# Decode attention over a sliding window with a gated feed-forward: units of one head or of two heads, runs of 24 KB or 48 KB per partition

## The chip, the cores and the metric

The kernel runs on one NeuronCore of a Trainium2 chip. The metric is the device time of one execution in microseconds. Five engines work side by side, each through its own list of instructions in order: TensorE (PE; its weight loads are shown as PEld), VectorE (DVE), ScalarE (ACT), GpSimd (POOL) and SyncE (SP), which here issues the transfers between the device memory (HBM) and the on-chip memory (SBUF). The transfers run on 16 DMA engines. Matrix products land in a second on-chip memory, PSUM.

## The reference

Four batches, one new position each. The 640-wide input is normalised, and two branches of it are added to the input: attention over the last W = 2,048 cached positions (32 heads of 192, every head with its own keys and values), and a SiLU-gated feed-forward of width 1,536. All data are bf16.

```python
B, Sq, D = 4, 1, 640
Hq, Hkv, Sk, Dh = 32, 32, 8192, 192
# k_cache, v_cache: (B, Hkv, Sk, Dh); wq: (D, Hq*Dh); wo: (Hq*Dh, D); w1, w3: (D, 1536); w2: (1536, D)
W = min(4096, max(256, Sk // 4))            # 2048
xn = layernorm(x)
q = (xn @ wq).reshape(B, Sq, Hq, Dh).transpose(0, 2, 1, 3)
k = k_cache[:, :, Sk - W:, :]; v = v_cache[:, :, Sk - W:, :]
p = softmax(einsum("bhqd,bhkd->bhqk", q, k) * Dh ** -0.5)
o = einsum("bhqk,bhkd->bhqd", p, v).transpose(0, 2, 1, 3).reshape(B, Sq, Hq * Dh) @ wo
h = silu(xn @ w1) * (xn @ w3)
out = x + o + h @ w2
```

Each key and each value is used once, so some 201 MB of cache pass through the core, and 22 MB of weights.

## The kernel before

The unit of work is a head of all four batches. `cache_rows` lays 2,048 positions of four batches on 128 partitions: partition q*4+b holds 64 neighbouring positions of batch b, one run of 64x192 bf16 = 24,576 bytes. `load_k` and `load_v` (L97, L102) move 3 MB each. Three key buffers and three value buffers stand ready (`KBUFS`, `VBUFS`); each wait for a free buffer is a wait of SP, ahead of everything that SP issues later.

A head is worked in four chunks of 16 positions per partition, one chunk per slot of a schedule. `mult` (L205, DVE) multiplies keys with the broadcast query into `pr`; `adder` (L215, PE) sums 192 products to 32 with six products against the identity, into one of two PSUM tiles `ps`; `reduce_tile` (L224, DVE) sums the 32. After the last chunk a chain finds the maximum of each batch: `lmax` (L231), a transpose (L236), `gmax` and `gmq` (L241, L244), a broadcast product (L250), `negm` (L252); then ACT takes the exponentials into `z` (L256), one instruction per batch and with a mask, so that each batch's row of `z` is zero on the other batches' partitions. `pv` (L275, PE) multiplies `z` with the values in 32 products of 32 columns, which go by turns to four column groups of PE; `fold` (L288, L292) adds the groups' rows and divides by the row sum of L262 and L264. Every four heads, `ge_tr` (L298) transposes the result, and `ge_proj` (L309) adds its product with 768 rows of `wo` into `acc`. The feed-forward comes last: gate and up (`ffn_mm`, L329), SiLU (L336), `ffn_transpose` (L346), `ff` (L406).

The order is written out by hand: `sched` holds, per slot (one chunk of keys, four per head) and phase, the functions to call. PE, DVE and ACT keep the order in which instructions are emitted, except that the build moves some forward between neighbours; SP issues in the order of the calls. These lines set what this text speaks of:

```python
if h >= KBUFS:
    add(s0 - (KBUFS - 1) * NC, 0, load_k, h)
add(s0 + L + NC * (1 - VBUFS), 0, load_v, h)
...
add(end - 2, 0, ffn_load, 1)
add(end - 2, 0, ffn_load, 3)
for n in range(NF):
    add(end, 0, w2_load, n)
add(end + L + 1, 7, ffn_mm, 1)
```

With `L` = 9, a head's products with the values begin nine slots after its first chunk. The query weights `wq` pass through the value buffers before the first values do. The gate weights go into key buffers behind the last heads' keys and behind the last V; `w2` follows them.

Of the kernel before, what the change touches and what calls it, by code (L numbers as in the profile page):

```python
# [18 lines left out]
def kernel(  # L19
# [16 lines left out]
    KBUFS: int = 3,  # L36
    VBUFS: int = 3,
    PBUFS: int = 4,
    NZ: int = 3,
    L: int = 9,  # L40
    RLAG: int = 2,
):

# [9 lines left out]
    NQ = P // B  # L53
# [6 lines left out]
    NS = H * NC  # L60
# [12 lines left out]
    assert H % (QP * NG) == 0 and NB <= 4  # L73
# [4 lines left out]
    vpool = ctx.enter_context(tc.tile_pool(name="vt", bufs=VBUFS))  # L78
    wpool = ctx.enter_context(tc.tile_pool(name="wstream", bufs=2))
# [10 lines left out]
    qbcs, wos, o_pss, rss, rcps, o_sbs, o_bfs, ges, chs = ({} for _ in range(9))  # L90
# [3 lines left out]
    def cache_rows(cache, h):  # L94
        return cache[:, h, Sk - W:Sk, :].rearrange("b (q n) d -> q b (n d)", q=NQ)

    def load_k(h):  # L97
        kt = kpool.tile([P, NJ, Dh], BF16, tag="kt")
        nc.sync.dma_start(out=kt[:], in_=cache_rows(A_k_cache, h))
        kts[h] = kt  # L100

    def load_v(h):  # L102
        vt = vpool.tile([P, NJ, Dh], BF16, tag="vt")
        nc.sync.dma_start(out=vt[:], in_=cache_rows(A_v_cache, h))
        vts[h] = vt

    def wo_load(hg):
        wt = wpool.tile([P, RPP * D], BF16, tag="w")
        nc.sync.dma_start(out=wt[:], in_=A_wo[hg * OW:(hg + 1) * OW, :].rearrange("(p i) n -> p (i n)", i=RPP))
        wos[hg] = wt  # L110

    x_sb = const.tile([B, D], BF16, name="x_sb")
    nc.sync.dma_start(out=x_sb[:], in_=A_x.rearrange("b s d -> (b s) d"))
    RV = NJ * Dh // (H * Dh)
    wq_rows = A_wq.rearrange("(p kc) n -> p kc n", kc=KC)
    wqs = []
    for r0 in range(0, KC, RV):
        r1 = min(r0 + RV, KC)
        wt = vpool.tile([P, RV, H * Dh], BF16, tag="vt")
        nc.sync.dma_start(out=wt[:, 0:r1 - r0, :], in_=wq_rows[:, r0:r1, :])  # L120
        wqs.append(wt)
    for h in range(KBUFS):
        load_k(h)
# [5 lines left out]
    ones_f = const.tile([P, 1], FP32, name="ones_f")  # L129
    nc.vector.memset(ones_f[:], 1.0)  # L130
    nsc = const.tile([1, B], FP32, name="nsc")
# [7 lines left out]
    rowsel = const.tile([P, 2 * B], FP32, name="rowsel")  # L139
    nc.vector.tensor_reduce(out=rowsel[:], in_=idf[:].rearrange("p (g c) -> p c g", g=NG)[:, 0:2 * B, :], axis=AX.X, op=ALU.add)  # L140
# [9 lines left out]
    sq = ppool.tile([B, D], FP32, tag="pr")  # L150
    ssq = const.tile([B, 1], FP32, name="ssq")
    nc.scalar.activation(out=sq[:], in_=xc[:], func=ACTF.Square, accum_out=ssq[:])
# [6 lines left out]
    xn = const.tile([B, D], BF16, name="xn")  # L159
# [8 lines left out]

    sel = const.tile([P, NQ, B], BF16, name="sel")
    nc.vector.tensor_copy(out=sel[:], in_=rowsel[:, 0:B].unsqueeze(1).to_broadcast([P, NQ, B]))  # L170
    selT = ps_t.tile([P, B], FP32, tag="t")
    nc.tensor.matmul(selT[:], lhsT=sel[0:B].rearrange("k q b -> k (q b)"), rhs=idb[0:B, 0:B], start=True, stop=True)
    mbias = const.tile([P, B], FP32, name="mbias")
# [19 lines left out]
    def q_bcast(qg):  # L193
        k, g = qg // NG, qg % NG
        bp = ps_t.tile([P, QW], FP32, tag="t")
        nc.tensor.matmul(bp[:], lhsT=sel[32 * g:32 * g + B].rearrange("k q b -> k (q b)"),  # L196
                         rhs=q_sb[32 * g:32 * g + B, k, :], start=True, stop=True)
        qbc = qpool.tile([P, QP, Dh], BF16, tag="qbc")
        nc.scalar.copy(out=qbc[:].rearrange("p h d -> p (h d)"), in_=bp[:])  # L199
        qbcs[qg] = qbc  # L200

    def mult(s):
        h, c = s // NC, s % NC
        pr = ppool.tile([P, CH, Dh], BF16, tag="pr")
        mi = nc.vector.tensor_tensor(out=pr[:], in0=kts[h][:, c * CH:(c + 1) * CH, :],  # L205
                                     in1=qbcs[h // QP][:, h % QP, :].unsqueeze(1).to_broadcast([P, CH, Dh]),
                                     op=ALU.mult)
        prs[s] = pr
        mult_insts[s] = mi
# [9 lines left out]
    def reduce_tile(s):  # L219
        h, c = s // NC, s % NC  # L220
        if c == 0:
            sc = small.tile([P, NJ], FP32, tag="sc", bufs=3)
            scs[h] = sc
        ri = nc.vector.tensor_reduce(out=scs[h][:, c * CH:(c + 1) * CH], in_=pss.pop(s)[:], axis=AX.X, op=ALU.add)  # L224
        ahead = min(s + RLAG, NS - 1)
        if ahead in mult_insts and ahead > s:
            tc.add_manual_dep(ri.ins, mult_insts[ahead].ins.name, ORDER_DEP, reason="vector engine issue order")

    def chain_lmax(h):
        lmax = small.tile([P, 1], FP32, tag="lmax")  # L230
        nc.vector.tensor_reduce(out=lmax[:], in_=scs[h][:], axis=AX.X, op=ALU.max)  # L231
        chs[h] = [lmax]

    def chain_tr(h):
        mt = ps_t.tile([P, P + B], FP32, tag="t")
        nc.tensor.transpose(out=mt[0:1, 0:P], in_=chs[h][0][:], identity=idf[:])  # L236
        chs[h].append(mt)

    def chain_gmax(h):
        gmax = small.tile([1, B], FP32, tag="gmax")  # L240
        nc.vector.tensor_reduce(out=gmax[:], in_=chs[h][1][0:1, 0:P].rearrange("o (q b) -> o b q", b=B),  # L241
                                axis=AX.X, op=ALU.max)
        gmq = small.tile([1, NQ, B], FP32, tag="gmq", bufs=1)
        nc.vector.tensor_copy(out=gmq[:], in_=gmax[:].unsqueeze(1).to_broadcast([1, NQ, B]))  # L244
        chs[h].append(gmq)

    def chain_bc(h):
        lmax, mt, gmq = chs.pop(h)
        sc = scs.pop(h)
        nc.tensor.matmul(mt[:, P:P + B], lhsT=gmq[:].rearrange("o q b -> o (q b)"), rhs=nsc[:], start=True, stop=True)  # L250
        negm = small.tile([P, B], FP32, tag="negm")
        nc.vector.tensor_tensor(out=negm[:], in0=mt[:, P:P + B], in1=mbias[:], op=ALU.add)  # L252
        z = zs[h % NZ][:].rearrange("p j (s b) -> p j s b", b=B)
        rs = small.tile([P, B], FP32, tag="rs")
        for b in range(B):
            nc.scalar.activation(out=z[:, :, 0:2, b], in_=sc[:].rearrange("p (j s) -> p j s", s=2), func=ACTF.Exp,  # L256
                                 bias=negm[:, b:b + 1], scale=SCALE, accum_out=rs[:, b:b + 1])
        rss[h] = rs

    def rowsum(h):  # L260
        tb = ps_t.tile([B, 1], FP32, tag="t")
        nc.tensor.matmul(tb[:], lhsT=rss.pop(h)[:], rhs=ones_f[:], start=True, stop=True)  # L262
        rcp = small.tile([B, 1], FP32, tag="rcp")
        nc.vector.reciprocal(out=rcp[:], in_=tb[:])  # L264
        rcps[h] = rcp

    def pv(s):
        h, c = s // NC, s % NC
        if c == 0:
            o_ps = ps_o.tile([P, 2 * Dh], FP32, tag="o_ps")  # L270
            o_pss[h] = o_ps
        o_ps, z, vt = o_pss[h], zs[h % NZ], vts[h]
        for jj in range(c * CH // 2, (c + 1) * CH // 2):
# [3 lines left out]
        if c == NC - 1:  # L277
            o_sb = opool.tile([P, 2, Dh], FP32, tag="o_sb")
            nc.scalar.copy(out=o_sb[:].rearrange("r two d -> r (two d)"), in_=o_pss.pop(h)[:])  # L279
            o_sbs[h] = o_sb  # L280
            vts.pop(h)

    def fold(h):
        hg, hl = h // HG, h % HG
        fp = ps_t.tile([B, Dh], FP32, tag="t")
        o_sb = o_sbs.pop(h)
        for two in range(2):
            nc.tensor.matmul(fp[:], lhsT=rowsel[:, two * B:(two + 1) * B], rhs=o_sb[:, two, :], start=(two == 0), stop=(two == 1))  # L288
        if hl == 0:
            o_bf = opool.tile([B, HG, Dh], BF16, tag="o_bf")  # L290
            o_bfs[hg] = o_bf
        nc.vector.tensor_scalar_mul(out=o_bfs[hg][:, hl, :], in0=fp[:], scalar1=rcps.pop(h)[:, 0:1])  # L292

    def ge_tr(hg):
        gp = ps_t.tile([P, RPP, B], BF16, tag="t")
        of = o_bfs.pop(hg)[:].rearrange("r h d -> r (h d)")
        for i in range(RPP):
            nc.tensor.transpose(out=gp[:, i, :], in_=of[:, i:OW:RPP], identity=idb[0:B, 0:B])  # L298
        oT = small.tile([P, RPP, B], BF16, tag="oT", bufs=2)
        nc.vector.tensor_copy(out=oT[:], in_=gp[:])  # L300
        ges[hg] = oT

    def ge_proj(hg, i):
        oT = ges[hg]
        wo_t = wos[hg]
        st = (hg == 0 and i == 0)
        sp = (hg == H // HG - 1 and i == RPP - 1)
        for t in range(2):
            nc.tensor.matmul(acc[32 * t:32 * t + B, :], lhsT=oT[:, i, :], rhs=wo_t[:, i * D + t * DH:i * D + (t + 1) * DH],  # L309
                             start=st, stop=sp)  # L310
# [3 lines left out]
    def ffn_load(which):  # L314
        wt = kpool.tile([P, KC, F], BF16, tag="kt")
        nc.sync.dma_start(out=wt[:], in_={1: B_w1, 3: B_w3}[which].rearrange("(p kc) n -> p kc n", kc=KC))
        ffn[which] = wt

    def w2_load(n):
        if n == 0:  # L320
            w2t = kpool.tile([P, NF, CF, D], BF16, tag="kt")
# [122 lines left out]
```

## Time and profile before

| | us |
|---|---|
| median of 3 runs (lowest, highest) | 529.62 (529.41, 531.23) |
| the profiled execution | 530.08 |
| its span | 528.3 |
| PE, DVE, ACT busy in it | 360.4, 340.3, 76.8 |
| DMA: bytes read, mean rate over the span | 222.96 MB, 422 GB/s |
| mean granted clock of TensorE | 0.848 of full |

The page cuts the span into 40 slices of 13.2 us; a table of stretches gives the same for any interval. A group's line holds the line of the kernel, the engine, the operation with what it writes and reads, the count, then busy time and mean duration, then the idle time of the engine just before them and what ended it. A line of waits reads: who waited, at which line, for what, in total, how often, the longest. The chain is followed back from the last instruction to what released it.

### The profile page before, as it was taken

The page shows a single profiled execution, that of the slowest core. Times are in us where ns is not written, and L with a number is a line of the kernel's source. Part 1 is how long each engine was busy: PE and PEld are TensorE (multiplying, and loading weights), DVE is VectorE, ACT ScalarE, POOL GpSimd, SP SyncE. Part 2 cuts the span into 40 slices and gives each one's busy share as a digit, 9 for nine tenths or more (in the row PEclk, how much of TensorE's full clock was granted, in tenths as well). Part 3 has the DMA queues.
Part 4 walks back from the last instruction along what each step waited for, and adds up shares of the span by engine and source line. Part 5 has one row for each costly group of instructions (what it writes and reads, how often), then busy time and mean ns, then how long its engine had stood idle before and what let it go on. Part 6 is the DMA issues. An engine that isn't in the chain of part 4 may idle for free.

```text
span 528.3 us, 5868 instructions
## 1 busy us (share of the span) xinstructions
PE 360.4 (68%) x2384; PEld 149.5 (28%) x2384; DVE 340.3 (64%) x477; ACT 76.8 (15%) x319; POOL 3.8 (1%) x11
## 2 busy tenths in 40 slices
PE   1456767877577777777566976767587775667765
PEld 1122222332222322223222322223232322223323
DVE  4069766677666657776566677766567776666702
ACT  2101111101111111011111110111111011111112
POOL 2000000000000000000000000000000000000000
PEclk9999988788777887878888787888878878788858
DMA  8999999999999999999999999999999999999994
GB/s 350 424 437 430 432 432 435 427 425 439 432 431 430 429 437 430 434 433 432 428 434 430 429 432 432 430 435 432 426 437 426 433 433 430 431 432 431 432 423 176
DMA packets 11562, 223.33 MB, mean 423 GB/s; under 512 B 1288, under 2 KB 1296, under 8 KB 2704
## 3 DMA queue, kind: packets, MB, share of 16 engines
q1 hardware_dynamic: 11536, 222.97, 98.4%
q8 instruction: 18, 0.29, 0.2%
q14 instruction: 8, 0.07, 0.0%
HBM read 222.96 MB, written 0.01 MB: 422 GB/s over the span
## 4 chain that ended last, share of the span: by engine, by line
DMA 59%; DVE 20%; PE 16%; ACT 3%; issue 1%; SPq 0%; DVEq 0%; ACTq 0%
DMA kt<-in_A_k_cache_dram 54%; DVE pr L205 14%; PE ps L215 10%; DMA vt<-in_A_v_cache_dram 5%; DVE sc L224 4%; PE o_ps L275 3%; ACT z L256 2%; PE acc L309 1%; ACT o_sb L279 1%; PE gt L329 0%; PE gp L298 0%; PE ff L406 0%; PE fp L288 0%; DVE lmax L231 0%; PE tb L262 0%
## 5 line engine op out<-in xcount | busy, mean ns | idle before, releaser
L215 PE MATMUL ps<-pr,idb 128*128 128x512 bf16 x768 | 239.5, 468 | 111.8 <-DVE sc L224 103.3
L205 DVE TENSOR_TENSOR pr<-kt,qbc 128x3072 bf16<-128x3072 bf16 x128 | 223.3, 1746 | 36.7 <-DMA kt<-in_A_k_cache_dram 36.5
L215 PEld LDWEIGHTS <-idb 128*128 128x128 bf16 x768 | 85.1, 114 | 240.3 <-issue 190.6
L224 DVE TENSOR_REDUCE sc<-ps 128x16 f32<-128x512 f32 x128 | 87.0, 680 | 0.6 <-PE ps L215 0.6
L275 PE MATMUL o_ps<-vt,z 128*32 128x384 bf16 x1024 | 56.7, 340 | 3.3 <-DMA vt<-in_A_v_cache_dram 3.3
L256 ACT ACTIVATE z<-sc,negm 128x64 bf16<-128x64 f32 x128 | 45.7, 423 | 89.7 <-DVE negm L252 89.7
L279 ACT COPY o_sb<-o_ps 128x384 f32<-128x384 f32 x32 | 15.1, 472 | 297.9 <-PE o_ps L275 297.9
L252 DVE TENSOR_TENSOR negm<-mt,mbias 128x4 f32<-128x4 f32 x32 | 5.2, 161 | 70.4 <-PE mt L250 70.4
L292 DVE TENSOR_SCALAR o_bf<-fp,rcp 4x192 bf16<-4x192 f32 x32 | 12.9, 405 | 56.1 <-PE fp L288 28.4
L288 PE MATMUL fp<-o_sb,rowsel 128*4 128x192 f32 x128 | 27.3, 338 | 14.6 <-ACT o_sb L279 14.6
L275 PEld LDWEIGHTS <-z 128*32 128x32 bf16 x1024 | 25.7, 98 | 28.5 <-issue 17.5
L256 ACT ACTIVATION_READ_ACCUMULATOR z<-sc,negm 128x1 f32 x128 | 23.9, 187 | 0.0
L288 PEld LDWEIGHTS fp<-o_sb,rowsel 128*4 128x4 f32 x128 | 8.6, 87 | 26.3 <-ACT o_sb L279 21.0
L262 PE MATMUL tb<-ones_f,rs 128*4 128x1 f32 x64 | 6.2, 166 | 12.9 <-ACT z L256 12.9
L250 PE MATMUL mt<-nsc,gmq 1*128 1x4 f32 x64 | 12.2, 258 | 1.3 <-DVE gmq L244 1.3
L250 PEld LDWEIGHTS mt<-nsc,gmq 1*128 1x128 f32 x64 | 9.4, 183 | 12.4 <-issue 10.4
L187 PE MATMUL qp<-wt,xnT 128*32 128x384 bf16 x80 | 7.0, 522 | 6.4 <-DMA wt<-in_A_wq_dram 6.4
L309 PE MATMUL acc<-wt,oT 128*4 128x320 bf16 x96 | 10.6, 307 | 0.6 <-DVE oT L300 0.5
L262 PEld LDWEIGHTS tb<-ones_f,rs 128*4 128x4 f32 x64 | 3.7, 86 | 23.6 <-ACT z L256 22.0
L236 PE MATMUL mt<-idf,lmax 128*1 128x128 f32 x32 | 9.7, 304 | 0.7 <-DVE lmax L231 0.4
L264 DVE RECIPROCAL rcp<-tb 4x1 f32<-4x1 f32 x32 | 4.9, 152 | 8.2 <-PE tb L262 8.2
L199 ACT CAST qbc<-bp 128x384 bf16<-128x384 f32 x16 | 7.6, 485 | 7.7 <-PE bp L196 7.7
(61 smaller groups left out, 81.4 us busy)
## 6 DMA issues: line engine op xcount, KB each, us to landing
kt<-in_A_k_cache_dram SPq DMA_DIRECT2D x32, 3072.0 KB, 36.6
vt<-in_A_v_cache_dram SPq DMA_DIRECT2D x32, 3072.0 KB, 40.3
wt<-in_A_wo_dram SPq DMA_DIRECT2D x8, 960.0 KB, 36.6
wt<-in_A_wq_dram SPq DMA_DIRECT2D x2, 3072.0 KB, 17.0
wt<-in_B_w_dram SPq DMA_DIRECT2D x2, 1920.0 KB, 32.0
w2t<-in_B_w_dram SPq DMA_DIRECT2D x3, 640.0 KB, 26.4
wt<-in_A_wq_dram SPq DMA_DIRECT2D x1, 1536.0 KB, 20.2
x_sb<-in_A_x_dram SPq DMA_DIRECT2D x1, 5.0 KB
```

What stands on the lines that cost most here:

```text
L205: mi = nc.vector.tensor_tensor(out=pr[:], in0=kts[h][:, c * CH:(c + 1) * CH, :], in1=qbcs[h // QP][:, h % QP, :].unsqueeze(1).to_broadcast ...
L215: nc.tensor.matmul(ps[:], lhsT=idb[:], rhs=pr[:, :, kk * DD:(kk + 1) * DD], start=(kk == 0), stop=(kk == NK - 1))
L224: ri = nc.vector.tensor_reduce(out=scs[h][:, c * CH:(c + 1) * CH], in_=pss.pop(s)[:], axis=AX.X, op=ALU.add)
L236: nc.tensor.transpose(out=mt[0:1, 0:P], in_=chs[h][0][:], identity=idf[:])
L250: nc.tensor.matmul(mt[:, P:P + B], lhsT=gmq[:].rearrange("o q b -> o (q b)"), rhs=nsc[:], start=True, stop=True)
L256: nc.scalar.activation(out=z[:, :, 0:2, b], in_=sc[:].rearrange("p (j s) -> p j s", s=2), func=ACTF.Exp, bias=negm[:, b:b + 1], scale=SCAL ...
L262: nc.tensor.matmul(tb[:], lhsT=rss.pop(h)[:], rhs=ones_f[:], start=True, stop=True)
L275: nc.tensor.matmul(o_ps[32 * g:32 * g + 32, :], lhsT=z[:, jj, :], rhs=vt[:, 2 * jj:2 * jj + 2, :], start=(jj < NG), stop=(jj >= NJ // 2 - NG))
L279: nc.scalar.copy(out=o_sb[:].rearrange("r two d -> r (two d)"), in_=o_pss.pop(h)[:])
L288: nc.tensor.matmul(fp[:], lhsT=rowsel[:, two * B:(two + 1) * B], rhs=o_sb[:, two, :], start=(two == 0), stop=(two == 1))
L292: nc.vector.tensor_scalar_mul(out=o_bfs[hg][:, hl, :], in0=fp[:], scalar1=rcps.pop(h)[:, 0:1])
L309: nc.tensor.matmul(acc[32 * t:32 * t + B, :], lhsT=oT[:, i, :], rhs=wo_t[:, i * D + t * DH:i * D + (t + 1) * DH], start=st, stop=sp)
```

## The change

The unit becomes a pair of heads, h and h+16, of all four batches: I = B*X = 8 rows, 16 units. `cache_rows` now puts 128 neighbouring positions on a partition (partition q*8+i, i = 2*b+x), a run of 49,152 bytes, and a load is 6 MB. Two key buffers and one value buffer take the place of three and three; they hold 96 KB and 48 KB per partition, before 72 and 72. The first four of five `wq` rows pass through the value buffer, the fifth through the `wo` buffer, of which there is one (before two), with two units' rows side by side. Eight chunks make a unit, and `pv` is called for the whole unit, in four parts, 16 slots after the unit's first chunk, that is behind the adders of the next unit. On SP, V(u) comes with the slot after the unit's last chunk, and K(u+2) one slot later. The last V is loaded in four parts.

At the end, gate and up weights are issued before the last V, into the buffer of the second last unit's keys, and their products, SiLU and transposes are called before the last unit's `pv`; the last `wo` load and `w2` come behind the last V. The projection's and `ff`'s products are 32 columns wide instead of 4, attention and input are added before `ff` is done, and one sum straight from PSUM ends it. The store goes out in two halves from SP and ACT, and the input is loaded by ACT, three small transfers, instead of SP. The query's broadcast is two accumulated products, one for each head of the pair. `ALIGN` pads a constant, so that the large buffers start at multiples of 512 bytes as before.

```diff
-    KBUFS: int = 3,
-    VBUFS: int = 3,
+    X: int = 2,
+    KBUFS: int = 2,
...
-    NZ: int = 3,
-    L: int = 9,
+    NZ: int = 2,
+    VP: int = 4,
...
-    NQ = P // B
+    U = H // X
+    I = B * X
+    NQ = P // I
...
-    vpool = ctx.enter_context(tc.tile_pool(name="vt", bufs=VBUFS))
-    wpool = ctx.enter_context(tc.tile_pool(name="wstream", bufs=2))
+    vpool = ctx.enter_context(tc.tile_pool(name="vt", bufs=1))
+    wpool = ctx.enter_context(tc.tile_pool(name="wstream", bufs=1))
...
-    def cache_rows(cache, h):
-        return cache[:, h, Sk - W:Sk, :].rearrange("b (q n) d -> q b (n d)", q=NQ)
+    def cache_rows(cache, u):
+        return cache.rearrange("b (x u) s d -> (b x) u s d", x=X)[:, u, Sk - W:Sk, :].rearrange(
+            "i (q n) d -> q i n d", q=NQ)
...
-    def load_v(h):
+    def load_v(u):
         vt = vpool.tile([P, NJ, Dh], BF16, tag="vt")
-        nc.sync.dma_start(out=vt[:], in_=cache_rows(A_v_cache, h))
-        vts[h] = vt
+        step = NJ if u < U - 1 else VC
+        for n in range(0, NJ, step):
+            nc.sync.dma_start(out=vt[:, n:n + step, :].rearrange("p n d -> p (n d)"),
+                              in_=cache_rows(A_v_cache, u)[:, :, n:n + step, :].rearrange("q i n d -> q i (n d)"))
+        vts[u] = vt
...
-    nc.sync.dma_start(out=x_sb[:], in_=A_x.rearrange("b s d -> (b s) d"))
+    nc.scalar.dma_start(out=x_sb[:], in_=x_rows)
...
-    for r0 in range(0, KC, RV):
...
+    for pool, tag, r0, r1 in ((vpool, "vt", 0, RV), (wpool, "w", RV, KC)):
+        wt = pool.tile([P, r1 - r0, H * Dh], BF16, tag=tag)
+        nc.sync.dma_start(out=wt[:], in_=wq_rows[:, r0:r1, :])
...
     def ffn_load(which):
-        wt = kpool.tile([P, KC, F], BF16, tag="kt")
+        if which == 1:
+            wt = kpool.tile([P, 3, KC * F], BF16, tag="kt")
+            ffn["w"] = wt
...
-    for h in range(H):
-        s0 = h * NC
-        if h >= KBUFS:
-            add(s0 - (KBUFS - 1) * NC, 0, load_k, h)
-        add(s0 + L + NC * (1 - VBUFS), 0, load_v, h)
+    add(-1, 0, load_v, 0)
+    for u in range(U):
+        s0 = u * NC
+        if u + 2 < U:
+            add(s0 + NC + 1, 0, load_k, u + 2)
+        if u:
+            add(s0 + NC, 8, load_v, u)
...
-            add(s + L, 3, pv, s)
...
+        for c in range(VP):
+            add(s0 + 2 * NC, 3, pv, u, c)
+        add(s0 + 2 * NC + 2, 6, fold, u)
...
+        add(a + (HG - 1) * NC + 2 if ug < U // HG - 1 else a + HG * NC + 1, 0, wo_load, ug)
...
-    add(end - 2, 0, ffn_load, 1)
-    add(end - 2, 0, ffn_load, 3)
+    add(end - NC + 1, 0, ffn_load, 1)
+    add(end - NC + 1, 0, ffn_load, 3)
     for n in range(NF):
-        add(end, 0, w2_load, n)
-    add(end + L + 1, 7, ffn_mm, 1)
-    add(end + L + 2, 7, ffn_mm, 3)
-    add(end + L + 3, 7, ffn_transpose)
+        add(end + 1, 1, w2_load, n)
+    add(end + 5, 7, ffn_mm, 1)
+    add(end + 6, 7, ffn_mm, 3)
+    add(end + 7, 7, ffn_transpose)
...
-    nc.scalar.copy(out=ffn_bf[:, 0:DH], in_=ff[0:B, :])
-    nc.vector.tensor_copy(out=ffn_bf[:, DH:D], in_=ff[32:32 + B, :])
-    res = ppool.tile([B, D], BF16, tag="pr")
-    nc.vector.tensor_tensor(out=res[:], in0=t1[:], in1=ffn_bf[:], op=ALU.add)
-    nc.sync.dma_start(out=out.rearrange("b s d -> (b s) d"), in_=res[:])
+    res = ppool.tile([64, DH], BF16, tag="pr")
+    nc.vector.tensor_tensor(out=res[:], in0=ff[:], in1=t1[:], op=ALU.add)
+    out_rows = out.rearrange("b s d -> (b s) d")
+    nc.sync.dma_start(out=out_rows[:, 0:DH], in_=res[0:B])
+    nc.scalar.dma_start(out=out_rows[:, DH:D], in_=res[32:32 + B])
```

## The prediction

> **What bounds the kernel now.** I read the page's first three parts, then the table of stretches, then the groups, the waits and the chain.
>
> ```profile
> PE 360.4 (68%) x2384; PEld 149.5 (28%) x2384; DVE 340.3 (64%) x477; ACT 76.8 (15%) x319; POOL 3.8 (1%) x11
> ...
> GB/s 350 424 437 430 432 432 435 427 425 439 432 431 430 429 437 430 434 433 432 428 434 430 429 432 432 430 435 432 426 437 426 433 433 430 431 432 431 432 423 176
> ...
> q1 hardware_dynamic: 11536, 222.97, 98.4%
> ```
>
> No engine is full, the one load queue is: 98.4% of 16 DMA engines' span. The stretches (busy us of PE, PEld, DVE, ACT, POOL; clock; DMA share; GB/s) show where it is not:
>
> ```profile
> 0.00:2.00 2.00, 0.00 (x0) 0.00 (x0) 0.20 (x3) 1.27 (x1) 1.45 (x9) 1.00 0.01 3
> ...
> 60.00:470.00 410.00, 292.93 (x1881) 119.63 (x1881) 280.42 (x385) 58.06 (x265) 0.00 (x0) 0.83 1.00 431
> ...
> 504.00:518.00 14.00, 9.51 (x83) 4.26 (x77) 1.06 (x4) 0.96 (x2) 0.00 (x0) 0.50 0.99 420
> 518.00:522.00 4.00, 2.17 (x27) 1.30 (x22) 0.24 (x1) 2.96 (x4) 0.00 (x0) 0.95 0.64 264
> ...
> 524.00:528.30 4.30, 0.84 (x14) 0.35 (x8) 0.98 (x3) 0.41 (x1) 0.00 (x0) 1.00 0.00 1
> ```
>
> So time can be won only before 2 us, after 523 us, or by moving the same 222.97 MB in less engine time. The next lines price the compute that the new order of loads waits for: groups first (busy, mean ns, idle before), then two stretches after a wait for keys, then waits, then pieces of the chain at the end.
>
> ```profile
> L215 PE MATMUL ps<-pr,idb 128*128 128x512 bf16 x768 | 239.5, 468 | 111.8 <-DVE sc L224 103.3
> L205 DVE TENSOR_TENSOR pr<-kt,qbc 128x3072 bf16<-128x3072 bf16 x128 | 223.3, 1746 | 36.7 <-DMA kt<-in_A_k_cache_dram 36.5
> ...
> L224 DVE TENSOR_REDUCE sc<-ps 128x16 f32<-128x512 f32 x128 | 87.0, 680 | 0.6 <-PE ps L215 0.6
> ```
> ```profile
> 288.20:296.50 8.30, 5.88 (x20) 2.15 (x20) 8.30 (x8) 0.00 (x0) 0.00 (x0) 0.59 0.99 427
> 296.50:304.00 7.50, 6.59 (x65) 3.01 (x65) 2.13 (x9) 1.87 (x9) 0.00 (x0) 1.00 1.00 429
> ```
> ```profile
> SPq L104 <- PE mt L250: 68.8, 22, 6.0
> ...
> SPq L104 <- PE o_ps L275: 22.2, 7, 3.2
> ```
> ```profile
> 509.72 2.78 PE o_ps L275 x31
> ...
> 516.44 2.27 PE gt L329 x10
> ...
> 523.05 1.84 PE ff L406 x24
> ```
>
> The reader is to see that DVE works 2.43 us per chunk of keys, that PE is at 0.59 of its clock after an idle stretch and then at 1.00, that V loads do wait for buffers but the queue never runs dry, and that the gate products stand behind the last V.
>
> **The load stream, term by term.** The trace's packet records give one length per size: 24,576 B take 912 ns, 15,360 B 573, 12,288 B 460, 7,680 B 291, 5,120 B 196. That is 36.8 ns per KB (1,000 B) and about 8 ns per packet. A load is 128 packets, 8 for each of the 16 engines. Before, per engine: wq 16x0.912+8x0.460=18.27; 64 key and value loads 64x8x0.912=466.94; wo 8x8x0.291=18.62; gate and up 16x0.573=9.17; w2 24x0.196=4.70; together 517.70. First packet at 2.13, sum 519.83; the last packet ended at 523.03 on the slowest engine. The 3.2 us between are slow first packets (up to 2.07 instead of 0.91) and instruction loads on the same engines; I keep them.
>
> - *48 KB packets.* Not in the trace. If the 8 ns are per packet, 49,152 B take 1.816: 31 loads x8x1.816=450.37, the last V in four pieces of 12,288 B 32x0.460=14.72, together 465.09, 1.85 less. wq saves 8x8 ns=0.06. Bounds: 0 (packets cut in two, 912 each) and 1.85; I take 1.85, since the five sizes lie on one line.
> - *x moved to ACT's queue.* wq becomes SP's first issue: 1.15 to 0.73, -0.42. The x loads are under 10 KB; the layer norm they feed ends at 9.4 and is wanted when wq lands (17 or later), so the rest costs nothing.
> - *One value buffer.* SP's order is now V(u), K(u+2), V(u+1), K(u+3); V(u+1) waits for the products of V(u), which PE does in order behind the adders of K(u+1). From K(u+1)'s last packet: 0.47 until an engine sees it (last V: packet end 509.25, PE 509.72); DVE up to the eighth mult's end 8x1.67+7x0.60 (start to start) =17.6, and lmax, o_bf, gmax, gmq, negm, rcp 1.4; then one reduce 0.60, the last adder 1.40 at full clock, 51 value matmuls at 46 ns (32 take 1.48) 2.35; then 0.98 from issue to first packet (1.15 to 2.13). Sum 24.8. The queue holds V(u) and K(u+2) meanwhile, 2x14.53=29.06. So 4.3 us of cover; I cost this at nothing. Bound if PE stayed at half clock (12 adder matmuls 5.28 us): 2.8+8x2.64+2.2+51x0.086+0.98=31.5, 2.4 late in each unit.
> - *K(u+2) behind V(u+1) on SP.* Its buffer is free after K(u)'s mults, before K(u+1)'s, so it never waits longer than the V issue ahead of it. wo loads stand between K and V three times and add 4.66 us cover there.
> - *Start.* V(0) waits for the q products (about 25 us) while K(0), K(1) run until 50. V(1)'s first packet by the same sum at about 77.5, K(2) ends at about 80: 2 us cover.
> - *Gate and up ahead of the last V.* There the queue holds V(14) and w1, w3: 14.53+9.17=23.70 against 24.8: dry for 1.1. Bounds 0.3 (an instruction load lengthens the stream) and 7.8 (half clock, 31.5). Taken: 1.2. With the half-clock rows only after idle stretches, and full clock from the third adder on, the low end is nearer.
> - *The end.* Before, 5.27 us follow the last packet (523.03 to 528.30): w2's landing meets the gate, SiLU and transpose chain at 523.05, then 24 ff matmuls, two casts, the sum and the store. After, hT is done long before; behind the last V come wo 4.66 and w2 4.70. With E the end of the last packet: last V at E-9.36, +0.47, 16 matmuls 1.38 at half clock, then o_sb, fold, o_bf, transposes, oT as before (512.57 to 515.75) 3.18, so acc begins at E-4.3; wo landed E-4.2; 24 acc matmuls, two column groups at a time, 1.7 to 3.2, done by E-1. The last third of ff after E+0.47: 0.61 (77 ns each) or 1.07; one sum 0.48 and handovers 0.08; from the sum's end to the span's end 2.32 as before. 3.96 to 5.0 where ff's first two thirds run late; I take 4.4: -0.87.
> - *Smaller rows.* Folds, max chains and row sums halve in number, exps stay 128 with twice the elements (ACT is at 15%), rows of z are wider but PV matmuls stay 1,024, mult and reduce stay 128. All of it lies beside the loads; without that cover it would be under 2 us a unit.
>
> Sum: -0.42-0.06-1.85+1.2-0.87=-2.0. Span 528.30 to 526.3, the profiled execution 530.08 to 528.1; it stands 0.46 above the median of the runs, 529.62, so **527.6**. That is 0.38% less. About 0.5% (2.65 us) is what a measurement of this kernel can tell from no change, so this counts as within.
>
> The Trainium skill's page "DMA: Bandwidth & Descriptors", section "Anatomy of one DMA", has a fixed cost of about 2.0 us per DMA (of those issued from GpSimd; here SP issues). No stretch from 60 to 470 us shows one (share 1.00 over 51 loads); where the queue runs dry, this rule in place of 0.98+0.47 would make the sum 0.6 us worse, 528.2.
>
> **Rivals.**
> 1. *The value buffer starves the queue (slower).* Place: SP's wait for V(u+1); price: whatever the chain takes beyond 29.06 us, times 11 units without cover from weights. For it: PE now idles some 7 us per unit, and after shorter idles the trace shows 0.59. Against: 1.00 from the third adder on, and 4.3 us of room. At half clock throughout 2.4x11=26, and the end's gap of 7.8: 527.6+26+6.6=560. It decides once a chunk takes over 0.54 us more than 2.27.
> 2. *The packets give nothing and the end is late.* Runs of 48 KB might move as two packets, and the gap may grow: 527.6+1.85 with no packet gain is 529.5, with a gap of 3 us 531.3. For it: no packet over 24,576 B is in the trace.
> 3. *Neighbouring partitions collide (slower).* The new order puts heads 48 MiB apart on neighbouring partitions, eight rather than four such streams. Nearest row: batches 96 MiB apart were read at 431 GB/s. Price by the slowest full-queue row, 406 GB/s (4 to 8 us): 201.3 MB take 496 instead of 467, 557 in all. The Trainium skill's page "DMA: Bandwidth & Descriptors", section "Latency and other measured facts", says large power-of-two row pitches can halve a copy's rate; the 431 disagrees for this layout.
> 4. *The end goes well.* Gap 0.3 and tail 3.96 give 527.6-0.9-0.44=526.3.
>
> **Chances.** Forecast 0.60 (own range 526.5 to 529.3, of which a quarter lies under 526.97, the 0.5% line); rival 1 0.07; rival 2 0.20 (a sixth of it over 532.27); rival 3 0.05; rival 4 0.08. Faster 0.15+0.08, say 0.24; slower 0.07+0.05+0.03=0.15; same 0.61. Range 526.0, under which only the luckier half of rival 4 lies, to 532.0, which leaves rivals 1 and 3 and the worst of 2 outside.
>
> **What would show it.** The record of key packets at about 1,816 ns; DMA share 1.00 in every unit and no SP wait that ends after K(u+2) landed; one dip of 1 to 2 us before the last V; the last packet near 522 and 4 to 5 us after it; ff's last matmuls behind w2, not behind hT. Key waits of DVE will be long in each unit (about 9 us) and cost nothing. Wrong would be: a dip in each unit (rival 1), packets of 912 ns (rival 2), packets over 1.9 us or GB/s under 425 with full share (rival 3).

## The result and the profile after

The changed kernel takes 1,024.67 us (median of 4 runs, 1,020.28 to 1,025.15), the kernel before 530.09 beside it (529.41 to 531.23): a ratio of 1.931, 95% interval 1.924 to 1.937. The forecast was 527.6, the range 526.0 to 532.0. It was wrong by 497 us.

The page of the changed kernel: engines, DMA share and rate in 40 slices, and the load queue.

```profile
span 1023.4 us, 5308 instructions
...
PE 367.8 (36%) x2216; PEld 145.0 (14%) x2216; DVE 320.0 (31%) x378; ACT 95.4 (9%) x294; POOL 5.2 (1%) x12
...
DMA  9999999999999999999999999999999999999997
GB/s 367 199 206 213 212 210 204 208 214 216 232 213 216 215 212 207 208 206 214 220 227 212 211 207 214 212 208 209 214 238 215 210 210 210 213 216 213 223 246 229
...
q1 hardware_dynamic: 7144, 222.96, 99.2%
```

PE and DVE are busy for about as long as before (DVE a little less, ACT with its wider exponentials a little more). The queue moves the same 222.96 MB, and it is still the bound, at 99.2%: the DMA engines never stop, they go at half speed. The table of stretches (busy us of PE, PEld, DVE, ACT, POOL; clock; DMA share; GB/s) shows from when on: 8 to 20 us are loads of `wq` (until 17.9 in packets of 49,152 B), 200 to 500 us are keys and values.

```profile
8.00:20.00 12.00, 2.32 (x30) 1.50 (x34) 1.66 (x9) 2.07 (x4) 0.00 (x0) 1.00 0.97 418
200.00:500.00 300.00, 108.52 (x641) 42.41 (x641) 96.83 (x111) 27.11 (x88) 0.00 (x0) 0.68 1.00 213
```

So the same size goes at two speeds. In the trace's packet records `wq`'s packets of 49,152 B took 1,815 ns, as forecast (1,816); the keys' and values' took 3,799 ns (medians). The waits say the same from the side of the engines:

```profile
DVE pr L231 <- DMA kt<-in_A_k_cache_dram: 624.3, 16, 45.7
```

DVE waits 624 us for keys, 16 times, where 36.5 us stood before. SP waits for buffers too, but the queue is never short of work meanwhile (share 1.00 from 200 to 500 us), so no wait of SP is behind it.

### The profile page after: what moved, and what is told of

Read it like the earlier page. It is cut to its first block, busy times and chain, and to the rows that moved or that the text cites. A ratio compares the mean times of both kernels' runs of the same rounds, so it can differ in the third digit from the quotient of the medians.

```text
span 1023.4 us, 5308 instructions
## 1 busy us (share of the span) xinstructions
PE 367.8 (36%) x2216; PEld 145.0 (14%) x2216; DVE 320.0 (31%) x378; ACT 95.4 (9%) x294; POOL 5.2 (1%) x12
## 3 DMA queue, kind: packets, MB, share of 16 engines
q1 hardware_dynamic: 7144, 222.96, 99.2%
HBM read 222.96 MB, written 0.01 MB: 218 GB/s over the span
## 4 chain that ended last, share of the span: by engine, by line
another core or an unknown queue 62%; DVE 20%; ACT 7%; PE 6%; DMA 3%; issue 1%; SPq 0%; DVEq 0%; ACTq 0%
DVE pr L231 13%; ACT z L282 7%; DVE sc L250 5%; PE ps L241 4%; DMA vt<-in_A_v_cache_dram 3%; PE fp L313 1%; PE o_ps L300 1%; DVE o_bf L317 0%; DVE xf L165 0%; PE acc L331 0%; PE tb L288 0%; PE ff L433 0%; DVE gmax L267 0%; DVE lmax L257 0%
## 5 line engine op out<-in xcount | busy, mean ns | idle before, releaser
L241 PE MATMUL ps<-pr,idb 128*128 128x512 bf16 x768 | 250.1, 481 | 435.9 <-DVE sc L250 405.5
L300 PE MATMUL o_ps<-vt,z 128*32 128x384 bf16 x1024 | 68.5, 414 | 161.0 <-DMA vt<-in_A_v_cache_dram 161.0
L282 ACT ACTIVATE z<-sc,negm 128x128 bf16<-128x128 f32 x128 | 74.4, 977 | 504.0 <-DVE negm L278 504.0
L300 PEld LDWEIGHTS <-z 128*32 128x32 bf16 x1024 | 33.2, 115 | 200.5 <-issue 183.7
L282 ACT ACTIVATION_READ_ACCUMULATOR z<-sc,negm 128x1 f32 x128 | 60.9, 476 | 0.0
L304 ACT COPY o_sb<-o_ps 128x384 f32<-128x384 f32 x16 | 7.7, 479 | 313.7 <-PE o_ps L300 313.7
L313 PE MATMUL fp<-o_sb,rowsel 128*8 128x192 f32 x64 | 14.5, 354 | 1.0 <-ACT o_sb L304 1.0
L317 DVE TENSOR_SCALAR o_bf<-fp,rcp 8x192 bf16<-8x192 f32 x16 | 6.4, 402 | 23.9 <-PE fp L313 23.8
L331 PE MATMUL acc<-wt,oT 128*32 128x320 bf16 x96 | 8.8, 343 | 0.3 <-DVE oT L324 0.3
L276 PE MATMUL mt<-nsc,gmq 1*128 1x8 f32 x32 | 6.1, 262 | 5.8 <-DVE gmq L270 5.8
```

The costliest lines, as they stand in the source:

```text
L241: nc.tensor.matmul(ps[:], lhsT=idb[:], rhs=pr[:, :, kk * DD:(kk + 1) * DD], start=(kk == 0), stop=(kk == NK - 1))
L276: nc.tensor.matmul(mt[:, P:P + I], lhsT=gmq[:].rearrange("o q i -> o (q i)"), rhs=nsc[:], start=True, stop=True)
L282: nc.scalar.activation(out=z[:, :, 0:2, i], in_=sc[:].rearrange("p (j s) -> p j s", s=2), func=ACTF.Exp, bias=negm[:, i:i + 1], scale=SCAL ...
L300: nc.tensor.matmul(o_ps[32 * g:32 * g + 32, :], lhsT=z[:, jj, :], rhs=vt[:, 2 * jj:2 * jj + 2, :], start=(jj < NG), stop=(jj >= NJ // 2 - NG))
L313: nc.tensor.matmul(fp[:], lhsT=rowsel[:, two * I:(two + 1) * I], rhs=o_sb[:, two, :], start=(two == 0), stop=(two == 1))
L317: nc.vector.tensor_scalar_mul(out=o_bfs[ug][:, ul, :], in0=fp[:], scalar1=rcps.pop(u)[:, 0:1])
```

## The experiments

**What halves the rate.** The change does three things to a load at once: runs of 48 instead of 24 KB; heads 48 MiB apart on neighbouring partitions; and a source pattern of 16 rows outside and 8 inside (16 x 8 runs) instead of 32 x 4. Four kernels take them apart. They keep all the work, but their output is not the reference's: the first two take keys and values from other rows, the last two take the right rows and match them to the wrong queries. In the first two the changed kernel's `cache_rows` is replaced, in the last two the kernel before's; the cuts show the new lines alone.

```diff
 # changed kernel, one constant step between the 128 runs
+rows = cache.rearrange("b h s d -> (b h s) d")
+return rows[u*18432:(u+1)*18432, :].rearrange("(p n) d -> p n d", p=P)[:, 0:NJ, :]
```

> The changed kernel, except that the 128 partitions of a load take 128 rows of 48 KB at one constant step in the cache (144 positions), a pattern of 128 x 24,576 elements instead of 16 x 8 x 24,576; it reads other cache rows than the reference asks for, all else is the same work. Theory A (the division of a load among the DMA engines follows the outer dimension of the source, and 16 x 8 makes pairs of engines meet at one place of SBUF): packets of 1,816 ns, full rate, and then the rest of the prediction holds: 527.6 us. Rival B (the memory addresses, neighbours 48 MiB apart and up to 192 MiB between batches, are what halves the rate): the addresses are gone here too, so also about 528. Rival C (runs of 48 KB in long succession are slow): stays near 1,020. If the single value buffer starves the queue at full rate, over 540.

```diff
 # changed kernel, the same region, 16 positions skipped after every 8th run: 16 x 8
+return rows[u*18688:(u+1)*18688, :].rearrange("(q m) d -> q m d", q=NQ)[:, 0:1152, :] \
+    .rearrange("q (i n) d -> q i n d", i=I)[:, :, 0:NJ, :]
```

> As the run before, with 16 positions left out after every eighth row, so that the source stays a pattern of 16 x 8 rows. Nearby addresses, no step of 48 MiB; again other rows than the reference's. Theory A: packets near 3,700 ns, about 1,020 us. Rival B: 528. Rival C: 1,020.

```diff
 # kernel before, runs of 24,576 B, heads 48 MiB apart on neighbours, 16 x 8
+rows = cache.rearrange("b (x u) s d -> (b x) u s d", x=2)[:, h % 16, Sk - W:Sk, :]
+return rows.rearrange("i (q t n) d -> q t i (n d)", q=16, t=2)[:, h // 16]
```

> The kernel before with its three and three buffers and its runs of 24,576 bytes, but each load takes 16 x 8 half runs of the changed kernel's layout (8 neighbours 48 MiB apart: four batches, two heads), so keys and queries are matched wrongly and the output is not the reference's; work and bytes are the same. Theory A: packets near 1,830 ns instead of 912, about 1,030 us. Rival B: slow as well, 900 to 1,030. Rival C: 530.

```diff
 # kernel before, runs of 24,576 B, heads 48 MiB apart on neighbours, 32 x 4
+rows = cache.rearrange("b (x u) s d -> (b x) u s d", x=2)[4*(h//16):4*(h//16)+4, h % 16, Sk-W:Sk, :]
+return rows.rearrange("i (q n) d -> q i (n d)", q=NQ)
```

> The kernel before, runs of 24,576 bytes as 32 x 4, but the four neighbours are two batches of two heads, 48 MiB apart instead of 96; keys and queries are matched wrongly, work and bytes are the same. Theory A: no change, 530 us, packets 912 ns. Rival B: slower, as far as the 48 MiB step is the cause, 600 to 1,000. Rival C: 530.

| load | time, us | key and value packets, median ns | GB/s, 200 to 500 us |
|---|---|---|---|
| 128 runs of 48 KB, constant step (4 runs) | 538.02 (1.0174 of before, 1.0116 to 1.0232) | 1,815 | 426 |
| nearby rows as 16 x 8 (1 run) | 1,030.26 | 3,802 | 213 |
| 24 KB, far neighbours, 16 x 8 (1 run) | 994.91 | 1,835 | 222 |
| 24 KB, far neighbours, 32 x 4 (1 run) | 530.39 (before: 530.60) | 912 | 431 |

The stretch from 200 to 500 us of the last two (columns as above), first 16 x 8, then 32 x 4:

```profile
200.00:500.00 300.00, 127.11 (x696) 50.50 (x696) 103.99 (x142) 21.24 (x95) 0.00 (x0) 0.69 1.01 222
```
```profile
200.00:500.00 300.00, 218.72 (x1397) 89.21 (x1396) 205.63 (x284) 41.37 (x189) 0.00 (x0) 0.82 1.00 431
```

Run length is not it (48 KB at full rate, 24 KB at half rate). The addresses are not it (far neighbours at 431 GB/s, near ones at half rate). The 16 x 8 pattern is, in every pair: a factor of nearly two, which single runs are enough to tell. The packets are as the first theory expected; the times are not in two places, 538.0 instead of 527.6 (taken up below) and 994.9 instead of some 1,030.

**Where the packets meet.** A pattern of 16 rows outside could be slow to read or slow to write. A kernel of loads alone puts the same rows at different partitions. In the cut, `phase(rows, lo, hi)` stands for a group of loads into partitions `lo` to `hi - 1`:

```diff
+phase(plain, 0, P)                      # (1) 128 runs
+phase(half, 0, P)                       # (2) 32 x 4 runs of 24,576 B
+phase(pair, 0, P)                       # (3) 16 x 8
+phase(one, 0, 64); phase(one, 32, 96); phase(one, 64, 128)   # (4) (5) (6) 16 x 4
+phase(rows64, 0, P)                     # (7) 64 x 2
+phase(rows8, 0, P)                      # (8) 8 x 16
```

> No computation: x is copied to the output, and key rows are loaded in eight successive groups of loads that nothing reads, each with another pattern, all but the second in runs of 49,152 B. (1) 128 rows in one run of memory; (2) the kernel before's 32 x 4 rows of 24,576 B; (3) the change's 16 x 8 rows; (4) 16 x 4 rows into partitions 0 to 63; (5) the same rows into partitions 32 to 95; (6) the same into 64 to 127; (7) 64 x 2; (8) 8 x 16. Theory A (16 rows outside give each DMA engine consecutive partitions, and engines four apart write the same way into SBUF at the same time): a packet takes 1.82, 0.91, 3.8, 3.6 to 3.8, 1.82 to 2.0, 3.6 to 3.8 us in (1) to (6); the sharp one is (5), where the same rows at another place in SBUF go at twice the rate of (4) and (6). Rival B (the slow side is the reading: memory, or the making of descriptors for 16 rows outside): (4), (5) and (6) alike, 3.6 to 3.8 if the pattern decides, 1.82 if it needs eight rows inside. (7) and (8) are open: 1.82 where engines are dealt groups of four partitions, 3.8 where they are dealt longer runs; in (8) A expects only 8 engines at work.

Its stretches, one per group in this order (POOL busy, clock, DMA share, GB/s):

```profile
10.00:58.00 48.00, 0.00 (x0) 1.00 1.00 431
62.00:88.00 26.00, 0.00 (x0) 1.00 1.01 432
100.00:200.00 100.00, 0.00 (x0) 1.00 1.01 212
215.00:295.00 80.00, 0.00 (x0) 1.00 0.98 200
308.00:342.00 34.00, 0.00 (x0) 1.00 0.98 425
355.00:430.00 75.00, 0.00 (x0) 1.00 1.01 206
445.00:490.00 45.00, 0.00 (x0) 1.00 1.01 436
510.00:715.00 205.00, 0.00 (x0) 1.00 0.50 111
```

Lines four to six are the sharp ones. The same 64 rows are read by the same pattern; into partitions 0 to 63 they go at 200 GB/s (3,847 ns a packet), into 32 to 95 at 425 (1,818 ns), into 64 to 127 at 206 (3,838 ns). So reading and describing the rows is not slow; where they are written decides, and rival B falls. With 16 x 8 all 128 partitions are written in the end, yet the rate is that of a load confined to half of them. The last line adds the count of engines: 8 rows outside put half of the engines to work (share 0.50), and their packets are slow too (3,767 ns).

The Trainium skill gives a reading of this. Its page "SBUF — State Buffer", section "Door 1: The DMA port swizzle (why `[64,N]` ≈ `[32,N]`)", maps partitions to 16 ports, groups of four partitions taking turns over eight of them in each half of 64, so that 32 partitions on have the same port; the trace agrees for lines four to six, whose rows reach 8, 16 and 8 ports by that map. Its page "DMA: Bandwidth & Descriptors", section "Why a DMA increments its semaphore by 16 and not by 1", divides a load over the largest number of engines, up to 16, that divides the slowest dimension of both patterns; the last line's 0.50 agrees. If each engine then takes one of the 16 outer rows, it writes eight consecutive partitions in order, and as long as the engines keep step, engines four apart write the same port at each moment: eight ports at a time, half of 431. That each engine does take one outer row is inferred from these rates; the records do not name a packet's engine. Nor can one rule of that kind be all: 64 x 2, dealt as four neighbouring rows to an engine, would give each engine eight consecutive partitions too, and line seven is fast (436 GB/s), as it would be if engines were dealt groups of four partitions. Shown is that pattern and place decide; how rows are dealt is not.

**What was left of the forecast.** At the full rate the change takes 538.0, not 527.6. In the first experiment's trace the queue runs dry four times (time lost, as a mean over the 16 engines): 3.2 us at 78, 0.4 at 353, 1.8 at 447 and 3.5 at 502. This piece of its timeline shows why V is late:

```profile
222.10 1.00 ACT L282 ACTIVATE z<-sc,negm 128x128 bf16<-128x128 f32 x1
...
223.16 0.20 PE L288 MATMUL tb<-ones_f,rs 128*8 128x1 f32 x2 [1.47 <-ACT z L282]
...
223.39 0.15 DVE L290 RECIPROCAL rcp<-tb 8x1 f32<-8x1 f32 x1 [1.12 <-PE tb L288]
```

The row sum `tb` (PE, with its reciprocal `rcp` on DVE) waits for the last of eight exponentials (0.54 us each from start to start, 128 elements wide; before 0.33 with 64), and PE and DVE, which keep their order, wait with it while chunks of the next keys are open. One edit moves it three slots on:

```diff
-        add(e + 6, 6, rowsum, u)
+        add(e + 9, 9, rowsum, u)
```

> The rows of 128 at a constant step (so again other data than the reference's, at the full rate), with the sum of the exponentials' rows three slots later. Theory: tb, which waits for the last exponential (ACTIVATE 128x128, a pitch of 0.54 us), stands in PE's order between two adders and holds the scores that free the key buffer and the products that free the one value buffer; taken out of the way, each V is issued 1.3 us earlier, and the dry stretches of 4.0, 0.4, 1.8 and 3.5 us become some 2.5, 0, 0.5 and 2.2: 533.5 us (532.5 to 535.5) against 538.0. Rival: the chain from K to V is that long whatever stands there, and tb only moves the wait: 537 to 539.

531.89 us (531.33 to 533.55; 1.0033 of before, 1.0019 to 1.0047, so within 0.5% of it): 6.1 less than with the early row sum, more than the 4.5 expected and a little under the expected range. From the first product with K to the issue of the next V it is now 203.74 to 226.90, 23.16 us, against 205.96 to 230.18, 24.22; over the units from the third on it is 22.91 to 23.64 against 24.14 to 26.70. The same unit shows which of the two waits went:

```profile
220.89 0.20 PE L288 MATMUL tb<-ones_f,rs 128*8 128x1 f32 x2 [1.04 <-ACT z L282]
...
222.80 0.15 DVE L290 RECIPROCAL rcp<-tb 8x1 f32<-8x1 f32 x1
```

On PE, `tb` still stands between two adders: it begins 17.15 us after the first product with K, before 17.20, and waits 1.04 us (before 1.47). What moved is the reciprocal. It no longer holds DVE, which had sat idle for it 1.12 us, so the last product with K starts 16.80 us after the first instead of 18.11, and V's issue follows 1.06 earlier. The expectation spoke of PE's order; the gain came from DVE's. Two dry places are left, 1.1 us at 78 and 2.5 before the last V:

```profile
78.00:83.00 5.00, 1.04 (x26) 0.52 (x18) 1.51 (x1) 0.48 (x1) 0.00 (x0) 0.98 0.82 288
495.00:500.00 5.00, 4.57 (x64) 2.20 (x62) 1.67 (x7) 0.48 (x1) 0.00 (x0) 1.00 0.54 189
```

**The start and the end alone.** The other parts of the change were put into the kernel before, with its 32 x 4 loads. First the whole start and end, but for the last V, which stayed in one piece:

```diff
-    nc.sync.dma_start(out=x_sb[:], in_=A_x.rearrange("b s d -> (b s) d"))
...
+    nc.scalar.dma_start(out=x_sb[:], in_=x_rows)
...
-    add(end - 2, 0, ffn_load, 1)
...
+    add(end - 4, 0, ffn_load, 1)
...
-    add(end + L + 1, 7, ffn_mm, 1)
...
+    add(end + L - 5, 7, ffn_mm, 1)
...
+    nc.vector.tensor_tensor(out=res[:], in0=ff[:], in1=t1[:], op=ALU.add)
```

> The kernel before with the start and the end of the change alone: x loaded through ACT's queue, the gate and up weights and their products ahead of the last V, accumulators 32 rows wide and one last sum from PSUM, the store in two halves on two queues. Loads of 24,576 B, three key and three value buffers as before. My terms: start -0.42, end 5.27 to 4.4 (-0.87), no gap ahead of the last V since three value buffers stay: 1.3 us under the kernel before, ratio 0.9975 (0.996 to 0.999). Rival: the end was hidden by the w2 transfers anyway: 0.9995 to 1.001.

It is slower, by a little more than either side expected: 531.63 us, 1.0021 of before (1.0009 to 1.0034). The end of its timeline:

```profile
518.71 2.75 PE L285 MATMUL o_ps<-vt,z 128*32 128x384 bf16 x32 [1.93 <-DMA vt<-in_A_v_cache_dram]
...
524.99 0.99 PE L318 MATMUL acc<-wt,oT 128*32 128x320 bf16 x12
...
527.47 0.35 SPq L419 DMA_DIRECT2D out_dram<-res  x1
```

The last packet (w2) has landed at 522.87, but the store goes out at 527.47, since 32 products at half clock, the copy, the fold, the projection and the sums follow the last V. Two kernels tell whether that is it. One keeps the order before at the end (last V, then gate, up, w2) with the new start and sums; the other is the one above with the last V in four pieces, as the change has it:

```diff
+        step = NJ if h < H - 1 else CH
+        for n in range(0, NJ, step):
+            nc.sync.dma_start(out=vt[:, n:n + step, :].rearrange("p n d -> p (n d)"), in_=cache_rows(A_v_cache, h)[:, :, n * Dh:(n + step) * Dh])
```

> The kernel before with the change's start (x through ACT's queue) and its last sum (accumulators 32 rows wide, one sum from PSUM, the store in two halves), but the order of the last loads and products as before: last V in one piece, then gate, up and w2. If the kernel with the whole end was slow because the last V came too late, this one gains what the shorter last sum saves, some 0.5 to 1.0 us: ratio 0.998 to 0.999. Rival: the shorter sum itself costs (wider accumulators, a second store): 1.001 to 1.003, as the kernel with the whole end.

> The kernel before with the change's start and end as in the kernel with the whole end (gate and up ahead of the last V), and the last V loaded in four pieces as the change has it. Theory: with V last but w2, the end is the chain from V's last packet (518.7) over 32 products at half clock (2.75), the copy (0.5), the fold (1.5), transposes, the last projection (1.0) and the sums; with four pieces only 8 products stand behind the last packet, 2 us less than the 1.0021 of one piece: ratio 0.997 to 0.9995. Rival: pieces move nothing, since PE's order or the fold decide: 1.001 to 1.003.

The first gives 529.88 us, 0.9994 (0.9984 to 1.0004): no difference that can be told, under what was expected. The second gives 528.76 us against 530.18, 0.9979 (0.9968 to 0.9991), so it is faster than the kernel before by 0.21%, or 1.1 us, where the one with V in one piece was slower by as much. Each was set against the kernel before run beside it, and both differences are small. Its end:

```profile
518.59 0.51 PE L287 MATMUL o_ps<-vt,z 128*32 128x384 bf16 x8 [1.32 <-DMA vt<-in_A_v_cache_dram]
...
521.69 0.99 PE L320 MATMUL acc<-wt,oT 128*32 128x320 bf16 x12
...
524.50 0.34 SPq L421 DMA_DIRECT2D out_dram<-res  x1
```

Eight products at full clock (granted clock 1.00) follow V's last packet instead of 32 at half clock (0.50), and the store goes out 2.97 us earlier. Without the pieces the new end was a loss.

## Why the prediction was wrong

- **The step that failed** stands in the load stream: "A load is 128 packets, 8 for each of the 16 engines", then "31 loads x8x1.816=450.37". The count per engine held; what failed is taking one duration per packet size for every load. The sizes' line came from patterns that all reach the full rate, and was carried to one that was not in the trace. At the median of 3,799 ns the term is 31x8x3.799=942, 492 us more; at the mean of 3,746, which is what adds up, 929, 479 more. The difference measured between the changed kernel and the same work with loads of 128 runs is 1,024.7-538.0=486.7. The bounds (0 and 1.85 of gain) left out a loss for no stated reason.
- **Rival 3** named the place, neighbouring partitions that collide, and its marks (packets over 1.9 us, GB/s under 425 at full share) are what the result shows. Its mechanism, heads 48 MiB apart in memory, is excluded: with them on neighbours the 32 x 4 loads ran at 431 GB/s, and rows of one region, eight inside, were as slow as heads far apart. Its price went by the slowest row of a full queue, 406 GB/s, so 557. The row that was needed, a load with 16 rows outside, the trace of before does not have. The 0.05 rested on addresses alone, though the diff shows the pattern change from 32 x 4 to 16 x 8. Of the rule on power-of-two pitches that the prediction cites there from the Trainium skill, the 431 is no exact test: 48 and 96 MiB are three times a power of two.
- **48 KB packets**: the price of one was right (1,815 ns against 1,816), the gain not in full. Over all packets an engine's sum fell from 521.30 to 520.33 us in the kernel with the late row sum, 0.97 of the forecast's 1.91: packets at the start and after each dry place are slow (up to 3,305 ns; the mean of this size is 1,824 against a median of 1,815).
- **x on ACT's queue**: the first packet of `wq` went from 2.13 to 1.75; -0.38 against -0.42.
- **One value buffer, in the steady units**: the forecast's chain without its first 0.47 and last 0.98 is 23.35. With the row sum late it took 23.16 (22.91 to 23.64 from the third unit on), so the arithmetic held; with the order as the change has it 24.22 (24.14 to 26.70). Missing was DVE's wait for the row sum, named in no step ("exps stay 128 with twice the elements (ACT is at 15%)" costed it at nothing by ACT's share, not by who stands behind it). The cover of 29.06 was enough in most units, and rival 1 did not come; the queue ran dry after the two longest, 26.70 (at 353) and 26.23 (at 447). Why a chain that is still under the cover left a gap there stays open.
- **The start**: instead of "2 us cover" there was a dry place of 3.2 us at 78 (1.1 with the late row sum). V(1)'s first packet was put at 77.5 "by the same sum", which from K(1)'s landing at about 50 would give 74.8; it came at 81.93. The step counts from the landing of K(1), but DVE was still on K(0)'s chunks until 54.4, and K(1)'s first product began at 54.87.
- **Gate and up ahead of the last V**: 1.2 forecast, 3.5 with the early row sum, 2.5 with the late one; inside the bounds of 0.3 and 7.8.
- **The end**: 4.4 forecast; 4.15 us from the last packet to the end in the first experiment (532.35 to 536.5), 4.16 with the late row sum. Right, and only with the last V in pieces, as the step had it: in one piece it was 7.1 (522.87 to 530.0).

So at the full rate the change would have been slower too, 538.0, outside the range by 6; about 6.1 us of that is the row sum's place. What is left, 531.89, lies in the range, but 0.33% over the kernel before and not 0.38% under it: the two dry places (3.6 us) take more than the start (0.4), the packets (1.0) and the end (1.1) win.

## What to carry to other kernels

A DMA's price is not set by its bytes and run length alone; its source pattern and the partitions that it writes can halve its rate. When a layout changes the outer dimension of a load (here 32 to 16), time a load of exactly that pattern, and bound an unseen pattern by a loss of half, or more where fewer engines work. A small instruction that waits for a slow engine should stand in the order where nothing that frees a buffer is queued behind it, and the trace tells on which engine it stands in the way. Moving a load to the end pays only if little work follows its last packet, so cut it into pieces.

## What was not expected of the hardware

- 64 partitions are written at 425 GB/s if they are 32 to 95, and at 200 to 206 if they are 0 to 63 or 64 to 127.
- A load over all 128 partitions can be as slow as one over half of them: 212 GB/s with 16 x 8 runs, 431 to 436 with 32 x 4, 64 x 2 or 128 runs. How rows are dealt to the engines the records do not show; only that 32, 64 and 128 reach the full rate.
- With 8 rows outside, the share is that of 8 engines (0.50), at 111 GB/s.
- Runs of 24,576 B with the slow pattern take 1,835 ns, twice 912, and runs of 49,152 B 3,799, 2.09 times 1,815.
- PE's mean granted clock was 0.848 before and 0.673 at half the load rate; the queue was the bound all the same (99.2%).
